# Weighing the last 64 rows of a head pair together with the 128 rows in front of them

## The chip, the cores and the metric

The kernel runs on one core of one Trainium2 chip. The metric is the device time of one execution in microseconds (us). Three runs of the kernel before gave 1619.87, 1620.59 and 1620.89 us, a median of 1620.59 us.

## The reference

Eight batches of eight heads, 576 rows, 64 columns per head. Each row of the scores keeps its 32 largest entries; the softmax of those weights the rows of v. The result feeds a gated FFN.

```python
scores = q @ k.T / sqrt(64)                    # (8, 8, 576, 576)
kth = 32nd largest of each row
scores = where(scores >= kth, scores, -1e9)
attn = softmax(scores)                         # exp(s - max) / (sum + 1e-9)
x = (attn @ v) -> (8 * 576, 512)
out = (sigmoid(x @ w_gate) * (x @ w_val)) @ w_out    # d_model 512, d_ff 1536
```

## The kernel before

Two heads are worked on together as a pair p (four pairs in a batch). A batch has 576 = 4 * 128 + 64 rows, so a pair has five row tiles: i = 0 to 3 of 128 rows for each of both heads, and i = 4, whose 64 rows of the one head and 64 rows of the other fill one tile of 128 partitions. Work goes in steps, one (group, pair, tile) each. `groups` (line 57) halves a batch: an even batch into tiles 0, 1, 2 and tiles 3, 4; an odd one into tiles 0, 1 and tiles 2, 3, 4. Each half is walked pair by pair.

A step loads queries (`ask`), makes scores on TensorE (PE) (`scores`, evicted by ScalarE (ACT), line 226), finds the 32nd largest value on VectorE (DVE) with ACT and GpSimd (POOL) (`select`), and makes masked numerators e and the reciprocal of their sum, inv, spread over the partitions (`masked`). Two steps later come the two functions of this change. `turn` transposes e on PE in chunks of 128 keys into PSUM tiles pt (two buffers, `ps_t`) and ACT copies these into the tile et, whose slots 0 to 3 hold the first head's keys, 5 to 8 the second's, and slot 4 the last 64 keys of both. A tile with i < 4 takes nine transposes (line 321) and three copies (line 322); the last one takes four transposes (326) and a copy of 128x512 (327), then one transpose (329) and a copy of 64 partitions (330). `weigh` multiplies et with the values vt into one PSUM bank po (one buffer, `ps_o`). For n of 128 or 256 columns: eight products with 64 weight columns, alternating between the upper and the lower half of the output partitions (lines 340, 341), and a full one with the mixed chunk (342). For the last tile, n = 64: eight such products (345, 346), then two of 64 rows by 64 columns, a quarter of the array each (347, 348). Products of float32 appear as two PE instructions each. Then inv is transposed into the same bank (351), ACT copies that to rs (354), DVE multiplies po by rs into xf (357, or twice on 64 partitions in 361), ACT makes the rounded part xh (364) and POOL the rest xl (365), in one or two pieces, as the units of 384 columns are cut.

The calls of `weigh` per pair: in an even batch tiles 0 and 1 together (n = 256), tile 2 (128), tile 3 (128), tile 4 (64); in an odd batch tiles 0 and 1 (256), tiles 2 and 3 (256), tile 4 (64). That makes 48 calls of 256 columns, 32 of 128 and 32 of 64 in all.

The FFN runs in twelve units of 384 columns (`ffn`, lines 396 to 398 for gate and val, 415 to 417 for the output). It is written into the program between the steps as a `goal` in worked columns allows, and the last unit after the last step. Weights are split into two parts in the first group of steps (`split_weight`). Within these data dependences the order of each engine's instructions is not that of the code: line 593 lets the tile framework order them by a timeline that it simulates while it builds the program.

Of the kernel before, what the change touches and what calls it, by code (L numbers as in the profile page):

```python
# [16 lines left out]
ALU = mybir.AluOpType  # L17
# [11 lines left out]
def tile_topk_attention_then_gated_ffn(  # L29
# [143 lines left out]
        return ks  # L173

    def load_values(b, p, nm):
        vt = bv.tile([P, 11, D], F32, tag="v", name=f"v_{nm}")
        nc.sync.dma_start(vt, v[b, p].rearrange("p (c d) -> p c d", d=D))
        return vt

# [133 lines left out]
    def turn(e, i, et, o, nm):  # L313

        ef = e.rearrange("p j s -> p (j s)")
        if i < NT:
            for g in range(3):
                pt = ps_t.tile([P, 4, P], F32, tag="t", name=f"pt_{nm}_{g}")
                for c in range(3):
                    k0 = (3 * g + c) * P  # L320
                    nc.tensor.transpose(pt[:, c], ef[:, k0 : k0 + P], ident)  # L321
                nc.scalar.activation(et[:, 3 * g : 3 * g + 3, o : o + P], pt[:, :3], AF.Copy)  # L322
        else:
            pt = ps_t.tile([P, 4, P], F32, tag="t", name=f"pt_{nm}_0")
            for c in range(4):
                nc.tensor.transpose(pt[:, c], ef[:, c * P : (c + 1) * P], ident)
            nc.scalar.activation(et[:, :4, :P], pt, AF.Copy)
            pt = ps_t.tile([P, 4, P], F32, tag="t", name=f"pt_{nm}_1")
            nc.tensor.transpose(pt[:REM, 0], ef[:, NT * P : S], ident)
            nc.scalar.activation(et[:REM, 4, :P], pt[:REM, 0], AF.Copy)  # L330

    def weigh(et, vt, n, invs, pieces, nm):

        both = ps_o.tile([P, 4 * P], F32, tag="o", name=f"po_{nm}")
        po, rb = both[:, :n], both[:, 2 * P :]
        if n > REM:
            mixed = vt[:, 4:6].rearrange("p a d -> p (a d)")

            for c in reversed(range(4)):
                nc.tensor.matmul(po[D:], vt[:, 6 + c], et[:, 5 + c, :n], start=c == 3, stop=False)  # L340
                nc.tensor.matmul(po[:D], vt[:, c], et[:, c, :n], start=c == 3, stop=False)
            nc.tensor.matmul(po, mixed, et[:, 4, :n], start=False, stop=True)  # L342
        else:
            for c in range(4):
                nc.tensor.matmul(po[:D], vt[:, c], et[:, c, :REM], start=c == 0, stop=False)
                nc.tensor.matmul(po[D:], vt[:, 6 + c], et[:, c, REM:P], start=c == 0, stop=False)
            nc.tensor.matmul(po[:D], vt[:REM, 4], et[:REM, 4, :REM], start=False, stop=True)
            nc.tensor.matmul(po[D:], vt[:REM, 10], et[:REM, 4, REM:P], start=False, stop=True)

        for t, inv in enumerate(invs):  # L350
            nc.tensor.transpose(rb[:, t * P : (t + 1) * P], inv, ident)  # L351
        rs = b2.tile([P, 2 * P], F32, tag="rs", name=f"rs_{nm}")
        m = len(invs) * P
        nc.scalar.activation(rs[:, :m], rb[:, :m], AF.Copy)
        xf = b2.tile([P, 2 * P], F32, tag="xf", name=f"xf_{nm}")[:, :n]
        if n > REM:
            nc.vector.tensor_tensor(xf, po, rs[:, :n], op=ALU.mult)
        else:
            for h in range(2):
                d = slice(h * D, h * D + D)  # L360
                nc.vector.tensor_tensor(xf[d], po[d], rs[d, h * REM : h * REM + REM], op=ALU.mult)
        o = 0
        for (xh, xl), c, k in pieces:
            nc.scalar.activation(xh[:, c : c + k], xf[:, o : o + k], AF.Copy)
            nc.gpsimd.tensor_tensor(xl[:, c : c + k], xf[:, o : o + k], xh[:, c : c + k], op=ALU.subtract)  # L365
            o += k
# [61 lines left out]
    def run(general):  # L428
        steps = [(g, p, i) for g, (_, first, end) in enumerate(groups) for p in range(NP) for i in range(first, end)]
        keys, values, qs, staged, xs = {}, {}, {}, {}, {}  # L430
        mark = "g" if general else ""

        def fetch(m):
            if m < len(steps) and steps[m][2] == groups[steps[m][0]][1]:
                g, p, _ = steps[m]
                b, first, _ = groups[g]
                if first == 0:
                    keys[b, p] = load_keys(b, p, f"{mark}{g}_{p}")
                values[g, p] = load_values(b, p, f"{mark}{g}_{p}")

        def begin(m):
            if m < len(steps):
                g, p, i = steps[m]
                staged[m] = scores(qs.pop(m), keys[groups[g][0], p], i, f"{mark}{groups[g][0]}_{i}_{p}")

        def ask(m):
            if m < len(steps):
                g, p, i = steps[m]
                qs[m] = load_queries(groups[g][0], i, p)

        for m in range(max(FETCH, ASK)):
            if m < FETCH:
                fetch(m)
            if m < ASK:
                ask(m)
        for m in range(AHEAD):
            begin(m)
        todo, work, at, col, unit = [], 0, 0, 0, 0
        parts, done = {}, {}

        for n in range(len(steps) + 2):
            if n < len(steps):
                g, p, i = steps[n]
                b, first, end = groups[g]
                m = n

                if not general and g == 0:
                    early, steps0 = LOADED + HELD, 3 * NP
                    for t in range(n * early // steps0, (n + 1) * early // steps0):
                        split_weight(order[t], t >= LOADED)  # L470
                        stored.add(order[t])
                fetch(n + FETCH)
                ask(n + ASK)
                begin(n + AHEAD)
                J = 2 if i < NT else 1
                nm = f"{mark}{b}_{i}_{p}"
                if general:
                    parts[n] = select_any(J, staged.pop(n), nm)
                else:
                    parts[n] = select(J, staged.pop(n), col, nm)  # L480
                next(parts[n])
                col += J
            if n - 1 in parts:
                done[n - 1] = next(parts.pop(n - 1))

            goal = max(at - BEHIND, min((at - U) * 1.5, U)) * 3 * (2 * NF * NP + NE * NF)
            while todo and work < goal:
                cost = next(todo[0], None)
                if cost is None:
                    todo.pop(0)  # L490
                else:
                    work += cost
            if n < 2:
                continue
            g, p, i = steps[n - 2]
            b, first, end = groups[g]
            nm = f"{mark}{b}_{i}_{p}"
            e, inv = done.pop(n - 2)
            if i == first or (i - first) % 2 == 0 or i == NT:
                et, o, invs = b2.tile([P, 9, 2 * P], F32, tag="et", name=f"et_{nm}"), 0, []  # L500
            turn(e, i, et, o, nm)
            invs.append(inv)
            o += P if i < NT else REM
            if len(invs) == 2 or i >= end - 1 or i == NT - 1:

                t, left, pieces = b * S + (i + 1 - len(invs)) * P, o, []
                while left:
                    u, c = t // U, t % U
                    if (u, p) not in xs:
                        if u % 3 == 2 and len(bxs) == 1:  # L510

                            for _ in todo.pop(0) if todo else ():
                                pass
                            split_done()
                        xs[u, p] = [bxs[u % 3 // 2].tile([P, U], F32R, tag=k, name=f"{k}{mark}_{u}_{p}") for k in ("xh", "xl")]
                    k = min(left, U - c)
                    pieces.append((xs[u, p], c, k))
                    t, left = t + k, left - k
                weigh(et, values[g, p], o, invs, pieces, nm)
            at += (P if i < NT else REM) / NP  # L520
            if p == NP - 1 and i == end - 1:
                while (unit + 1) * U <= b * S + min(end * P, S):
                    todo.append(ffn(f"{mark}{unit}", [xs[unit, d] for d in range(NP)], unit * U, general))
                    unit += 1
        for rest in todo:
            for _ in rest:
                pass
# [69 lines left out]
```

## Time and profile before

| | before |
|---|---|
| median of 3 runs | 1620.59 us |
| profiled execution | 1619.79 us |
| its span, first to last instruction | 1618.0 us |
| PE busy | 1553.3 us (96%) |
| DVE busy | 1265.3 us (78%) |
| POOL busy | 1206.8 us (75%) |
| ACT busy | 1168.9 us (72%) |
| mean granted PE clock | 0.981 of full speed |

A busy time is the sum of the times in which an engine had an instruction in work. Matmuls are pipelined: the record of one lasts longer than the distance to the next, so what one costs a full PE is read from the chain of waits, where a piece runs from the end of the piece before it to its own end.

### The profile page before, as it was taken

The page shows a single profiled execution, that of the slowest core. Times are in us where ns is not written, and L with a number is a line of the kernel's source. Part 1 is how long each engine was busy: PE and PEld are TensorE (multiplying, and loading weights), DVE is VectorE, ACT ScalarE, POOL GpSimd, SP SyncE. Part 2 cuts the span into 40 slices and gives each one's busy share as a digit, 9 for nine tenths or more (in the row PEclk, how much of TensorE's full clock was granted, in tenths as well). Part 3 has the DMA queues.
Part 4 walks back from the last instruction along what each step waited for, and adds up shares of the span by engine and source line. Part 5 has one row for each costly group of instructions (what it writes and reads, how often), then busy time and mean ns, then how long its engine had stood idle before and what let it go on. Part 6 is the DMA issues. An engine that isn't in the chain of part 4 may idle for free.

```text
span 1618.0 us, 33444 instructions
## 1 busy us (share of the span) xinstructions
PE 1553.3 (96%) x10226; PEld 1391.1 (86%) x10226; DVE 1265.3 (78%) x5748; ACT 1168.9 (72%) x2615; POOL 1206.8 (75%) x1923
## 2 busy tenths in 40 slices
PE   5878999899999999999999999999999999999998
PEld 2434897789999999999999999989999999999998
DVE  5999878988888779887888778888788778888300
ACT  6888778977777777777777777777777777777322
POOL 3679977897767896787877886788876996776413
PEclk9878999999999999999999999999999999999999
DMA  7556745665655565565555665655565665554575
GB/s 240 191 187 223 262 166 190 208 217 207 220 191 187 197 247 198 207 227 204 200 193 189 222 234 188 218 175 206 202 200 181 217 225 197 187 200 165 194 268 178
DMA packets 88989, 331.98 MB, mean 205 GB/s; under 512 B 9952, under 2 KB 36576, under 8 KB 61920
## 3 DMA queue, kind: packets, MB, share of 16 engines
q1 hardware_dynamic: 88800, 329.75, 59.0%
q8 instruction: 83, 1.36, 0.3%
q14 instruction: 106, 0.87, 0.2%
HBM read 301.40 MB, written 28.31 MB: 204 GB/s over the span
## 4 chain that ended last, share of the span: by engine, by line
PE 75%; POOL 7%; DVE 4%; ACT 3%; issue 1%; DMA 1%; POOLq 0%; SPq 0%; ACTq 0%
PE pz L396 11%; PE pz L397 11%; PE pz L398 11%; PE pss L219 8%; PE pt L321 6%; PE po L340 6%; PE po L415 5%; PE po L417 5%; PE po L416 5%; POOL u L302 3%; PE po L342 2%; DVE e L238 1%; PE po L351 1%; POOL k L171 1%; DVE kths L310 1%
## 5 line engine op out<-in xcount | busy, mean ns | idle before, releaser
L302 POOL TENSOR_TENSOR u<-s,under 128x288 f32<-128x288 f32 x576 | 444.5, 794 | 83.3 <-ACT under L296 77.3
L284 DVE MAX8 cand<-s 128x8 f32<-128x72 f32 x2304 | 348.1, 218 | 73.4 <-ACT s L226 63.3
L396 PE MATMUL pz<-xh,w 128*128 128x384 f32 x1120 | 383.9, 344 | 0.5 <-ACT gf L401 0.5
L397 PE MATMUL pz<-xl,w 128*128 128x384 f32 x1120 | 380.1, 339 | 0.3 <-POOL xl L365 0.3
L398 PE MATMUL pz<-xh,w 128*128 128x384 f32 x1120 | 379.5, 339 | 0.0
L238 DVE SCALAR_TENSOR_TENSOR e<-s,kths,e 128x576 f32<-128x576 f32 x288 | 291.7, 1020 | 2.8 <-ACT e L233 2.7
L310 DVE MAX8 kths<-u 128x8 f32<-128x584 f32 x288 | 219.6, 763 | 88.5 <-POOL u L303 86.3
L296 ACT ACTIVATE under<-s,leads 128x576 bf16<-128x576 f32 x288 | 223.4, 777 | 43.1 <-DVE leads L288 38.1
L233 ACT ACTIVATE e<-s,st 128x576 f32<-128x576 f32 x288 | 210.1, 774 | 52.0 <-POOL st L292 51.3
L404 POOL TENSOR_TENSOR gl<-gf,gh 128x384 fp32r<-128x384 f32 x144 | 156.0, 1084 | 92.4 <-ACT gh L403 90.3
L322 ACT ACTIVATE et<-pt 128x384 f32<-128x384 f32 x384 | 179.8, 490 | 46.4 <-PE pt L321 45.8
L396 PEld LDWEIGHTS pz<-xh,w 128*128 128x128 f32 x1120 | 210.8, 188 | 1.7 <-ACT gf L401 1.0
L397 PEld LDWEIGHTS pz<-xl,w 128*128 128x128 f32 x1120 | 211.4, 189 | 1.0 <-POOL xl L365 0.6
L398 PEld LDWEIGHTS pz<-xh,w 128*128 128x128 f32 x1120 | 211.1, 189 | 0.0
L226 ACT ACTIVATE s<-pss 128x576 f32<-128x576 f32 x256 | 164.5, 643 | 42.1 <-PE pss L219 41.4
L416 PE MATMUL po<-gl,w 128*128 128x384 f32 x560 | 189.5, 340 | 0.4 <-POOL gl L404 0.3
L415 PE MATMUL po<-gh,w 128*128 128x384 f32 x560 | 188.8, 350 | 0.9 <-ACT acc L419 0.9
L321 PE MATMUL pt<-ident,e 128*128 128x128 f32 x1152 | 184.9, 279 | 4.9 <-DVE e L238 2.6
L417 PE MATMUL po<-gh,w 128*128 128x384 f32 x560 | 187.4, 338 | 0.0
L321 PEld LDWEIGHTS pt<-ident,e 128*128 128x128 f32 x1152 | 144.7, 143 | 28.9 <-DVE e L238 6.5
L219 PE MATMUL pss<-k,qh 128*128 128x288 f32 (+2 forms) x588 | 167.5, 303 | 2.0 <-ACT s L226 2.0
L219 PE MATMUL pss<-k,ql 128*128 128x288 f32 (+2 forms) x588 | 159.1, 293 | 0.0
(105 smaller groups left out, 3318.6 us busy)
## 6 DMA issues: line engine op xcount, KB each, us to landing
w<-ws SPq DMA_DIRECT2D x210, 1024.0 KB, 4.9
v<-in_v_dram SPq DMA_DIRECT2D x64, 352.0 KB, 3.3
wraw<-in_w_dram SPq DMA_DIRECT2D x36, 512.0 KB, 4.4
ws<-wsplit SPq DMA_DIRECT2D x36, 512.0 KB, 3.5
qraw<-in_q_dram SPq DMA_DIRECT2D x140, 128.0 KB, 3.0
kraw<-in_k_dram SPq DMA_DIRECT2D x56, 288.0 KB, 3.8
out_dram<-acc SPq DMA_DIRECT2D x48, 192.0 KB, 4.0
q<-in_q_dram SPq DMA_DIRECT2D x20, 128.0 KB, 3.5
```

Source lines behind the costliest of these rows:

```text
L219: nc.tensor.matmul(ps[:, half, o : o + n], x[:K, h * P : (h + 1) * P], ks[h][:K, k0 : k0 + n], start=t == 0, stop=t == len(todo) - 1,)
L238: nc.vector.scalar_tensor_tensor(e[:, j], s[:, j], kth[j], e[:, j], op0=ALU.is_ge, op1=ALU.mult, accum_out=st[:, 4 + j : 5 + j])
L284: nc.vector.max(cand[:, j, 8 * g : 8 * g + 8], s[:, j, g * SEG : (g + 1) * SEG])
L302: nc.gpsimd.tensor_tensor(u[:, j, c], s[:, j, c], under[:, j, c], op=ALU.mult)
L310: nc.vector.max(kths[:, at[j] : at[j] + 8], u[:, j])
L321: nc.tensor.transpose(pt[:, c], ef[:, k0 : k0 + P], ident)
L396: nc.tensor.matmul(ps, wt[:, u, 0, d], xh, start=d == 0, stop=False)
L397: nc.tensor.matmul(ps, wt[:, u, 0, d], xl, start=False, stop=False)
L398: nc.tensor.matmul(ps, wt[:, u, 1, d], xh, start=False, stop=d == NP - 1)
L415: nc.tensor.matmul(ps, wt[:, e % 2, 0, f], gh, start=f == 0, stop=False)
L416: nc.tensor.matmul(ps, wt[:, e % 2, 0, f], gl, start=False, stop=False)
L417: nc.tensor.matmul(ps, wt[:, e % 2, 1, f], gh, start=False, stop=f == FG - 1)
```

## The change

The last tile no longer has a weigh call of its own. Its transposes are written behind the 128 columns of tile 3 in the same et, and one call weighs 192 columns. Tile 2 of an odd batch, which shared a call with tile 3, is weighed alone. The calls per pair become 256, 128 and 192 columns in every batch, 32 of each in all. For the last tile to have the layout of the others, `turn` copies each half of the 128 rows to the slots of its head (two copies of 128 partitions by 4 times 64), transposes the last 128 key columns once more as a whole, and copies 64x64 of each of the last two transposes to slot 4. The values lose their eleventh chunk, which was a second copy of the second head's first 64 rows at partitions 0 to 63.

```diff
-        vt = bv.tile([P, 11, D], F32, tag="v", name=f"v_{nm}")
+        vt = bv.tile([P, 10, D], F32, tag="v", name=f"v_{nm}")
...
-            nc.scalar.activation(et[:, :4, :P], pt, AF.Copy)
+            for h in range(2):
+                nc.scalar.activation(et[:, 5 * h : 5 * h + 4, o : o + REM], pt[:, :, h * REM : h * REM + REM], AF.Copy)
             pt = ps_t.tile([P, 4, P], F32, tag="t", name=f"pt_{nm}_1")
             nc.tensor.transpose(pt[:REM, 0], ef[:, NT * P : S], ident)
-            nc.scalar.activation(et[:REM, 4, :P], pt[:REM, 0], AF.Copy)
+            nc.tensor.transpose(pt[:, 1], ef[:, S - P : S], ident)
+            for h in range(2):
+                d = slice(h * D, h * D + D)
+                nc.scalar.activation(et[d, 4, o : o + REM], pt[d, h, h * REM : h * REM + REM], AF.Copy)
...
-        if n > REM:
-            mixed = vt[:, 4:6].rearrange("p a d -> p (a d)")
-
-            for c in reversed(range(4)):
-                nc.tensor.matmul(po[D:], vt[:, 6 + c], et[:, 5 + c, :n], start=c == 3, stop=False)
-                nc.tensor.matmul(po[:D], vt[:, c], et[:, c, :n], start=c == 3, stop=False)
-            nc.tensor.matmul(po, mixed, et[:, 4, :n], start=False, stop=True)
-        else:
-            for c in range(4):
-                nc.tensor.matmul(po[:D], vt[:, c], et[:, c, :REM], start=c == 0, stop=False)
-                nc.tensor.matmul(po[D:], vt[:, 6 + c], et[:, c, REM:P], start=c == 0, stop=False)
-            nc.tensor.matmul(po[:D], vt[:REM, 4], et[:REM, 4, :REM], start=False, stop=True)
-            nc.tensor.matmul(po[D:], vt[:REM, 10], et[:REM, 4, REM:P], start=False, stop=True)
+        mixed = vt[:, 4:6].rearrange("p a d -> p (a d)")
+
+        for c in reversed(range(4)):
+            nc.tensor.matmul(po[D:], vt[:, 6 + c], et[:, 5 + c, :n], start=c == 3, stop=False)
+            nc.tensor.matmul(po[:D], vt[:, c], et[:, c, :n], start=c == 3, stop=False)
+        nc.tensor.matmul(po, mixed, et[:, 4, :n], start=False, stop=True)
...
-        if n > REM:
-            nc.vector.tensor_tensor(xf, po, rs[:, :n], op=ALU.mult)
-        else:
+        f = n // P * P
+        nc.vector.tensor_tensor(xf[:, :f], po[:, :f], rs[:, :f], op=ALU.mult)
+        if n > f:
             for h in range(2):
                 d = slice(h * D, h * D + D)
-                nc.vector.tensor_tensor(xf[d], po[d], rs[d, h * REM : h * REM + REM], op=ALU.mult)
+                nc.vector.tensor_tensor(xf[d, f:], po[d, f:], rs[d, f + h * REM : f + h * REM + REM], op=ALU.mult)
...
-            if i == first or (i - first) % 2 == 0 or i == NT:
+            if i == NT - 1 or (i < NT and (i - first) % 2 == 0):
                 et, o, invs = b2.tile([P, 9, 2 * P], F32, tag="et", name=f"et_{nm}"), 0, []
...
-            if len(invs) == 2 or i >= end - 1 or i == NT - 1:
+            if len(invs) == 2 or i == end - 1 or i == NT - 2:
...
-    vl = np.zeros((B, H // 2, P, 11, D), v.dtype)
+    vl = np.zeros((B, H // 2, P, 10, D), v.dtype)
...
-    vl[:, :, :R, 10] = vb[:, :, :R]
-    vl = vl.reshape(B, H // 2, P, 11 * D)
+    vl = vl.reshape(B, H // 2, P, 10 * D)
```

## Rows read from the trace of the kernel before

**Rows 1.** Busy time of each engine in three stretches of the span: start and end, length, then busy us and number of instructions for each engine, the granted PE clock, the DMA share and GB/s.

```profile
0.00:200.00 200.00, 156.76 (x727) 93.27 (x728) 171.23 (x747) 158.20 (x325) 142.84 (x233) 0.87 0.66 221
200.00:1530.00 1330.00, 1315.29 (x9038) 1217.94 (x9037) 1086.87 (x4987) 990.85 (x2249) 1039.58 (x1666) 1.00 0.58 202
1530.00:1618.00 88.00, 81.21 (x465) 79.88 (x463) 7.24 (x15) 19.81 (x42) 24.35 (x25) 0.99 0.62 222
```

**Rows 2.** The waits of PE between 200 and 1530 us: who waited for whom, us in total, times, longest.

```profile
PE pt L321 <- ACT et L322: 2.2, 1, 2.2
...
PE po L340 <- DVE xf L357: 1.7, 1, 1.7
```

**Rows 3.** The chain of waits through a weigh call of 256 columns, in order of time: start, us, engine, tile, line. After it one transpose of the last tile and the next FFN product.

```profile
1521.60 0.36 PE po L340
1521.97 0.21 PE po L340
...
1523.48 0.63 PE po L342 x2
1524.11 0.22 PE po L351 x2
1524.33 0.11 PE pt L329
1524.44 0.18 PE pz L397
```

**Rows 4.** The same chain through a call of 128 columns.

```profile
824.72 0.25 PE po L340
...
825.74 0.42 PE po L342 x2
826.16 0.11 PE po L351
826.27 0.27 PE pss L219 x2
```

**Rows 5.** The same chain through a call of 64 columns.

```profile
1480.67 0.20 PE po L345
1480.87 0.05 PE po L345
...
1481.28 0.20 PE po L347
...
1481.54 0.26 PE po L351
1481.80 0.66 PE pt L321 x6
```

**Rows 6.** The quarter-array products of line 347 in the first two of the same three stretches: PE busy us and count, weight loads, clock, DMA share, GB/s. A call has two of them.

```profile
0.00:200.00 200.00, 0.33 (x2) 0.19 (x2) 0.87 0.66 221
200.00:1530.00 1330.00, 10.06 (x62) 5.82 (x62) 1.00 0.58 202
```

**Rows 7.** Groups of instructions by line and shape: line, engine, operation, tiles, shapes, count | busy us, mean ns of one | idle before, releaser. First PE, then the weight loads of line 340.

```profile
L329 PE MATMUL pt<-ident,e 128*64 128x128 f32 x32 | 8.7, 272 | 0.0
L340 PEld LDWEIGHTS po<-et,v 128*64 128x64 f32 x640 | 77.2, 139 | 43.6 <-issue 10.7 <-ACT et L322 3.0 <-DVE xf L357 2.0
```

**Rows 8.** The same view for ACT, DVE and POOL.

```profile
L327 ACT ACTIVATE et<-pt 128x512 f32<-128x512 f32 x32 | 19.0, 595 | 5.4 <-PE pt L326 5.4
L330 ACT ACTIVATE et<-pt 64x128 f32<-64x128 f32 x32 | 8.4, 261 | 0.0
L354 ACT ACTIVATE rs<-po 128x256 f32<-128x256 f32 x48 | 18.2, 379 | 20.2 <-PE po L351 20.1
L354 ACT ACTIVATE rs<-po 128x128 f32<-128x128 f32 x64 | 17.3, 270 | 15.7 <-PE po L351 15.3
L364 ACT ACTIVATE xh<-xf 128x64 fp32r<-128x64 f32 x48 | 12.2, 257 | 12.1 <-DVE xf L361 12.0
L364 ACT ACTIVATE xh<-xf 128x128 fp32r<-128x128 f32 x32 | 10.0, 313 | 10.5 <-DVE xf L357 10.5
L364 ACT ACTIVATE xh<-xf 128x192 fp32r<-128x192 f32 x16 | 5.9, 370 | 2.4 <-DVE xf L357 2.1
L357 DVE TENSOR_TENSOR xf<-po,rs 128x128 f32<-128x128 f32 x32 | 8.8, 276 | 1.6 <-ACT rs L354 1.5
L365 POOL TENSOR_TENSOR xl<-xf,xh 128x64 fp32r<-128x64 f32 x48 | 20.2, 421 | 4.4 <-ACT xh L364 3.6
L365 POOL TENSOR_TENSOR xl<-xf,xh 128x192 fp32r<-128x192 f32 x16 | 10.5, 659 | 1.5 <-ACT xh L364 1.0
```

**Rows 9.** The DMA of the values (queue, count, KB each, median us from issue to landing).

```profile
v<-in_v_dram SPq DMA_DIRECT2D x64, 352.0 KB, 3.3
```

**Rows 10.** The timeline of POOL after the last weigh call: start, us, line, tiles.

```profile
1532.08 0.32 POOL L365 TENSOR_TENSOR xl<-xf,xh 128x64 fp32r<-128x64 f32 x1
```

**Rows 11.** The chain of waits at the first product of the last FFN unit.

```profile
1535.67 0.17 PE pz L396
```

**Rows 12.** ACT in order of time near a weigh call of 64 columns: start, us, line, tiles [idle before, releaser].

```profile
1480.15 0.78 ACT L296 ACTIVATE under<-s,leads 128x576 bf16<-128x576 f32 x1 [0.43 <-DVE leads L288]
```

## The prediction

> **What bounds the kernel now.** I read first how the busy time lies in the span. In the first 200 us PE is busy 156.76 of 200 and DVE 171.23: several engines wait for each other there, and time taken from PE is worth little. From 200 to 1530 us PE is busy 1315.29 of 1330 us at a granted clock of 1.00, while DVE has 1086.87, POOL 1039.58 and ACT 990.85 [rows 1]. What fills PE there sets the end; the other engines have 243, 290 and 339 us to spare. After 1530 us only the FFN is left. Second, PE's waits in the long stretch: its whole idle time is 1330 - 1315.3 = 14.7 us, and the waits that touch this change happened once each, 2.2 us for a copy into et and 1.7 us for xf [rows 2]. Third, the chain of waits through the calls. This view is needed because the mean of a PE record is no price: the transpose of line 329 lasts 272 ns by its record [rows 7], but its piece of the chain is 0.11 us, and the product behind it has 0.18 us [rows 3]. So every PE price below is a stretch of the chain, from the start of a call's first piece to the start of what follows the call.
>
> **Where the calls lie.** Of the 64 quarter-array products of line 347, two to a call, 2 lie before 200 us and 62 after [rows 6]. So 31 of the 32 small calls stand where PE is full, and one, of batch 0, does not. I count nothing for that one.
>
> **PE, the calls.**
> - 256 columns with two transposes of inv: 1521.60 to 1524.33, 2.73 us [rows 3].
> - 128 columns with one: 824.72 to 826.27, 1.55 us [rows 4].
> - 64 columns with one: 1480.67 to 1481.80, 1.13 us [rows 5]. Much of it isn't work on columns. The first piece is 0.20 where a later one of line 345, with its partner, is 0.06; the first quarter product is 0.20 again; the transpose behind it is 0.26 where 0.11 is usual. That is 0.14 + 0.14 + 0.15 = 0.43 us for three changes of how the array is divided. A call without quarters has two of them: 0.36 for 0.21 at its start and 0.63 for 0.43 at line 342, 0.15 + 0.20 us [rows 3].
> - 192 columns with two transposes of inv: not in the trace. Without the transposes the calls of 256 and 128 cost 2.73 - 0.22 = 2.51 and 1.55 - 0.11 = 1.44; both have the same 18 products and the same two changes, so what differs is the columns, and 192 is the mean, 1.975. With two transposes 2.195 us. The ends are the two neighbours, 1.44 + 0.22 = 1.66 and 2.73. I take the mean, because the price of a piece goes with its columns (0.06, 0.11, 0.21 for 64, 128, 256).
>
> Even batch, per pair: before 1.55 + 1.13 = 2.68, after 2.195, a gain of 0.485. Odd batch: before 2.73 + 1.13 = 3.86, after 1.55 + 2.195 = 3.745, a gain of 0.115; the columns are the same 320, only the changes of the array go, and one call more ends on the dear line 342. Sum: 15 * 0.485 + 16 * 0.115 = 7.3 + 1.8 = 9.1 us.
>
> **PE, the added transpose.** One more full transpose for each last tile, 31 * 0.11 = 3.4 us by the chain [rows 3]. The nearest row from the other side is the record, 0.272 us [rows 7], 8.4 us. I take 0.11, since in the chain the next product is not late behind it. Net on PE: 9.1 - 3.4 = 5.7 us gained.
>
> The Trainium skill speaks against this choice: its page "TensorE: Matmul & The Clock Gate" (Part 4: PE-mode transpose) measures about 275 ns for a 128x128 transpose in a kernel's context. By that price the sum would be 9.1 - 31 * 0.275 = 0.6 us. The record in this trace agrees with the page (272 ns), the distance to the next product (0.11 us) does not.
>
> **ACT.** Per last tile, copies of 595 and 261 ns go [rows 8]. In their place come two copies of 256 elements a partition, for which the nearest is rs of that size, 379 ns, and two of 64 elements, at most the 257 ns of xh 128x64: 1272 for 856 ns, 0.42 us, 13.3 us in all. In an even batch a copy of rs of 379 stands for two of 270, and one of xh of 370 for 313 and 257 [rows 8]: 16 * 0.36 = 5.8 us less. Net 7.5 us of ACT, hidden in its 339 spare us; if ACT were the bound, it would cost that. Below: its records overlap at their ends, so 0 is possible. I take nothing.
>
> **DVE, POOL.** In an odd batch the product po * rs is cut in two, at most one more of 276 ns, 16 * 0.28 = 4.4 us of DVE [rows 8] against 243 spare. POOL has one xl less per pair of an even batch. Both hidden; nothing, with ends of 0 and 4.4 us.
>
> **The values.** Each of 64 loads shrinks by a tenth of 3.3 us at the most [rows 9], 0.3 us each. They are issued two steps ahead, and PE has no wait for them between 200 and 1530 us. Their queue, SP, carries nothing new. Nothing, with at most a few us of gain in the first 200 us as the other end.
>
> **The wait that is added.** Tile 3 is now weighed only when tile 4 has been transposed and copied, one step later. Behind a weigh call that comes too early stand, on PE, the next FFN products and the next transposes, and behind those ACT's copies. But et has two buffers and needs no more of them than before, and the FFN of those columns is put into the program only after the group's last pair. At the very end the last xl is done at 1532.08 + 0.32 = 1532.40 [rows 10], and the last FFN unit starts at 1535.67 [rows 11]: 3.27 us of slack. The last call is later by 2.195 - 1.13 = 1.07 on PE, 0.11 for the transpose, 0.42 for the copies, 0.11 for rs, 0.28 on DVE, 0.11 for xh and 0.24 for xl [rows 8]: 2.3 us. It fits, with 0.9 us left.
>
> **The sum.** The profiled execution took 1619.79 us, 1.79 more than its span. Less 5.7 that is 1614.1 us. The median of the runs is 0.8 us above the profiled one, so I predict 1614.9 us. By the ends of the transposes alone (0.11 or 0.272 us) it is 1614.9 to 1619.9 us. A call of 192 at its lower end of 1.66 us would give 31 * 0.535 = 17 us more, one at 2.73 us would take as much; both would need 64 columns to be free or dear as 128, against all three sizes, and stay outside the range.
>
> **Rivals.**
> - *The transposes cost their records.* Then 9.1 - 8.4 = 0.7 us is left and the time is 1619.9 us, no change. For it: 272 ns [rows 7]. Against it: the chain [rows 3]. Chance 0.06.
> - *The new order of the program gives the gain back.* The tile framework orders the instructions by its own simulated timeline, and every price in that has changed a little. PE's 14.7 us of idle time are made of waits that happened once or a few times [rows 2], accidents of one order. With 4 us more of them the time is 1618.9 us, no change measured. Against it: it can as well lose some of them. Chance 0.18.
> - *The call of 192 waits for its own tile.* Place: PE at the first product of line 340, since the order was laid for one copy of 64 partitions and now four copies stand behind whatever ACT has begun. Price: a piece of ACT such as the sign pass of 0.78 us [rows 12]; at every second call 16 * 0.78 = 12.5 us, time 1614.9 + 12.5 = 1627.4 us, slower. It eats the whole gain from 5.7 / 32 = 0.18 us per call and makes the kernel measurably slower from (5.7 + 3.2) / 32 = 0.28 us. Against it: so far the weight loads of line 340 waited 3.0 us for et in 80 calls, 0.04 us a call [rows 7]. Chance 0.08.
> - *The change does not do what it says:* one PE piece of a last tile too many or few would show in the counts; I see none in the diff and give it no chance of its own.
>
> **How the numbers follow.** My forecast has 0.68, with a range of its own of 1610 to 1617 us: an order that loses 4 to 5 us of the idle time below, one that adds 2 above. A measurement of this kernel tells about 0.2% from no change, 3.2 us. The forecast is faster by more than that (below 1617.3). The rivals of the transposes and of the order, 0.24 together, lie within 0.2%; the waiting call, 0.08, is slower. The range for 8 in 10 goes from 1609.5 to 1621 us: it takes in both rivals without a change and leaves out the slower one and the far ends of the order.
>
> **What would show it.** Right: lines 345 to 348 gone, the chain through a call of 192 columns near 2.2 us with its two transposes, the added transpose at 0.11 us of chain, PE busy between 200 and 1530 us still at 99% with the same FFN work, and the last unit's start some 5.7 us earlier. Wrong: a wait of PE or its weight loads at line 340 for et that is counted in tens, a call of 192 that is well above 2.2 us, or named waits of PE that add up to 4 us more than before although the calls are as cheap as worked out; then the order and not the operations decided.

## The result, and the profile after

The changed kernel took 1629.74 us in the median of 6 runs (1627.32 to 1634.33), the kernel before, on the same chip beside it, 1620.74 us. The ratio is 1.0052 (95% interval 1.0034 to 1.0070): slower by 8.4 us where 5.7 us of gain were forecast. The profiled execution took 1627.84 us, its span is 1626.0 us.

The same three stretches of the span as in [rows 1], of the changed kernel (PE, weight loads, DVE, ACT, POOL, then the granted clock):

```profile
0.00:200.00 200.00, 153.11 (x675) 88.36 (x676) 167.30 (x731) 154.75 (x320) 137.68 (x226) 0.87 0.66 215
200.00:1530.00 1330.00, 1308.06 (x8717) 1216.24 (x8716) 1092.68 (x5016) 993.25 (x2284) 1033.60 (x1656) 0.99 0.58 200
1530.00:1626.00 96.00, 89.24 (x518) 87.02 (x516) 7.99 (x17) 21.09 (x44) 25.98 (x27) 0.98 0.61 224
```

PE is idle 21.9 us between 200 and 1530 us where it was 14.7, and 46.9 us before 200 us where it was 43.2. Over the whole span PE is busy 1550.4 us (1553.3 before): it does a little less, and it stands 10.9 us more (75.6 us for 64.7).

First the priced pieces. The chain of waits through a call of 192 columns, to be held against [rows 3, 4]:

```profile
1511.44 0.31 PE po L343
1511.75 0.01 PE po L344
1511.76 0.16 PE po L343
...
1512.89 0.52 PE po L345 x2
1513.42 0.22 PE po L348 x2
1513.64 0.66 PE pt L321 x6
```

From 1511.44 to 1513.64 it takes 2.20 us; 2.195 were worked out. The same chain through the last tile's transposes (line 331 is the added one), and the group of the added ones:

```profile
1504.74 0.44 PE pt L326 x4
1505.18 0.11 PE pt L330
1505.29 0.11 PE pt L331
```

```profile
L331 PE MATMUL pt<-ident,e 128*128 128x128 f32 x32 | 8.7, 272 | 0.0
```

Again 0.11 us in the chain under a record of 272 ns. The Trainium skill's figure of about 275 ns (page "TensorE: Matmul & The Clock Gate", Part 4: PE-mode transpose) agrees with the record of one and not with what one more of them costs a full PE.

Summed over the trace, each PE record from the end of the one before to its own end, idle time left out, the products and inv transposes of `weigh` take 213.7 us for 224.9, and the added transposes 3.5: the operations are 7.7 us cheaper. So the time must have gone to waits and to the clock. The longest waits of PE, over the whole span:

```profile
PE wrest L146 <- DVE wraw L139: 15.9, 8, 6.0
PE pt L321 <- DVE e L238: 11.1, 6, 5.1
PE pss L203 <- DMA q<-in_q_dram: 6.4, 1, 6.4
PE pt L321 <- ACT et L322: 5.7, 7, 1.3
PE pss L219 <- ACT s L226: 5.5, 9, 2.0
...
PE po L343 <- ACT et L322: 1.3, 3, 0.5
...
PE po L343 <- ACT et L328: 0.7, 1, 0.7
```

The same rows of the kernel before:

```profile
PE pt L321 <- DVE e L238: 2.6, 4, 0.8
PE pt L321 <- ACT et L322: 2.2, 1, 2.2
PE pss L219 <- ACT s L226: 2.0, 2, 1.8
```

No call waits for its own tile to any account: line 343 waits 2.0 us for et in four places. What grew are the waits of transposes and scores for the attention's other engines: in the kernel before the transposes waited 2.2 us for et and the scores 2.0 us for s (once or twice), now 5.7 and 5.5 us in 7 and 9 places. The largest growth, of the transposes' wait for e from 2.6 to 11.1 us, lies in the first 200 us, where other waits shrank. By stretches PE's idle time grew by 3.7 us before 200 us, by nothing from 200 to 345 us and by 7.3 us from 345 to 1600 us.

The places show more; the largest growth in one of them after 345 us lies near 1420 us. Busy times in stretches of 10 us there, the changed kernel first, then the kernel before:

```profile
1410.00:1420.00 10.00, 10.00 (x70) 9.14 (x66) 7.41 (x32) 7.88 (x19) 7.27 (x13) 1.00 0.56 183
1420.00:1430.00 10.00, 8.00 (x50) 7.00 (x50) 8.13 (x41) 6.16 (x14) 8.52 (x15) 0.91 0.52 180
1430.00:1440.00 10.00, 8.07 (x54) 5.78 (x51) 8.67 (x44) 7.78 (x18) 5.10 (x12) 0.84 0.18 49
```

```profile
1420.00:1430.00 10.00, 10.00 (x66) 8.39 (x65) 6.97 (x36) 6.39 (x15) 9.31 (x16) 1.00 0.80 253
1430.00:1440.00 10.00, 10.00 (x66) 9.89 (x65) 9.13 (x48) 6.99 (x16) 4.59 (x10) 1.00 0.67 238
```

In 20 us PE stands 3.9 us, and the clock is granted at 0.91 and 0.84, means of its two levels of 2.4 and 1.2 GHz (1.00 and 0.50). The chain of waits through that place:

```profile
1421.99 0.24 DVE leads L288
...
1422.32 0.87 ACT under L296 x2
1423.18 0.76 ACT et L322 x2
1423.94 0.84 ACT e L233 x2
...
1425.16 0.86 ACT under L296 x2
1426.02 0.30 ACT qh L188
1426.33 0.55 ACT s L226
...
1426.92 1.48 PE pss L219 x10
1428.40 0.62 PE po L343
1429.02 0.01 PE po L344
1429.02 0.42 PE po L343
```

For a while the chain isn't on PE: ACT works off a queue, PE waits 2.0 us for one of its copies, then a piece of 256 columns takes 0.42 us where 0.21 is usual [rows 3], that is, 1.2 GHz for 2.4.

Why here: the columns of FFN unit 10 reach into tiles 0 and 1 of batch 7, so it needs the 256-column calls of all four pairs. PE in order of time, the changed kernel first (unit 10's first product, the first score product after the wait, the call of the fourth pair, the next product of unit 10), then the kernel before:

```profile
1418.03 0.33 PE L393 MATMUL pz<-xh,w 128*128 128x384 f32 x1
...
1426.92 0.40 PE L219 MATMUL pss<-k,qh 128*128 128x288 f32 x1 [2.00 <-ACT s L226]
...
1428.33 0.69 PE L343 MATMUL po<-et,v 128*64 128x256 f32 x1
...
1436.45 0.79 PE L393 MATMUL pz<-xh,w 128*128 128x384 f32 x3 [1.25 <-ACT xh L361]
```

```profile
1420.59 0.33 PE L396 MATMUL pz<-xh,w 128*128 128x384 f32 x1
...
1422.24 0.43 PE L340 MATMUL po<-et,v 128*64 128x256 f32 x1
```

Before, the fourth pair's call follows 1.7 us after unit 10's first product. In the changed kernel it follows 10.3 us after; by 1424.6 us PE has done the 27 FFN products that three pairs allow (three PSUM tiles, nine products each). Then no FFN work is left, and PE hangs on DVE, ACT and POOL, step by step. Counted in the trace, PE has done 1266 score products when unit 10 starts at 1420.6 us in the kernel before, but only 1248 when it starts at 1418.0 us in the changed kernel: the FFN has run further ahead of the attention. After a third of unit 10 both have done 1304 score products, at 1462.0 and at 1469.6 us: the stretch is 10.2 us longer, partly by the 18 score products and what follows from them, and by 3.9 us idle and (0.09 + 0.16) * 10 = 2.5 us of clock.

### The profile page after: what moved, and what is told of

It reads as the page before. It is cut to its first block, busy times and chain, and to the rows that moved or that the text cites. A ratio compares the mean times of both kernels' runs of the same rounds, so it can differ in the third digit from the quotient of the medians.

```text
span 1626.0 us, 32812 instructions
## 1 busy us (share of the span) xinstructions
PE 1550.4 (95%) x9906; PEld 1391.6 (86%) x9906; DVE 1268.0 (78%) x5764; ACT 1169.1 (72%) x2647; POOL 1197.3 (74%) x1907
## 3 DMA queue, kind: packets, MB, share of 16 engines
q1 hardware_dynamic: 88800, 327.65, 58.5%
## 4 chain that ended last, share of the span: by engine, by line
PE 59%; DVE 11%; POOL 10%; ACT 10%; issue 3%; DMA 3%; POOLq 0%; SPq 0%; ACTq 0%; DVEq 0%
PE pz L394 9%; PE pz L395 9%; PE pz L393 9%; PE pss L219 7%; PE po L343 5%; PE pt L321 4%; POOL u L302 4%; PE po L412 4%; PE po L413 4%; PE po L414 4%; DVE e L238 3%; DVE kths L310 3%; DVE cand L284 2%; ACT e L233 2%; ACT under L296 2%
## 5 line engine op out<-in xcount | busy, mean ns | idle before, releaser
L302 POOL TENSOR_TENSOR u<-s,under 128x288 f32<-128x288 f32 x576 | 438.8, 784 | 103.1 <-ACT under L296 99.0
L238 DVE SCALAR_TENSOR_TENSOR e<-s,kths,e 128x576 f32<-128x576 f32 x288 | 296.0, 1033 | 3.8 <-ACT e L233 2.0
L401 POOL TENSOR_TENSOR gl<-gf,gh 128x384 fp32r<-128x384 f32 x144 | 153.0, 1064 | 89.5 <-ACT gh L400 86.4
L321 PE MATMUL pt<-ident,e 128*128 128x128 f32 x1152 | 181.9, 279 | 17.0 <-DVE e L238 11.1
```

Source lines behind the costliest of these rows:

```text
L238: nc.vector.scalar_tensor_tensor(e[:, j], s[:, j], kth[j], e[:, j], op0=ALU.is_ge, op1=ALU.mult, accum_out=st[:, 4 + j : 5 + j])
L302: nc.gpsimd.tensor_tensor(u[:, j, c], s[:, j, c], under[:, j, c], op=ALU.mult)
```

## The experiments

Theories: the order of the instructions (C), the joined call itself (D), and as a first form of C the shorter load of the values (A), since the order differs from that of the kernel before from 33 us on, long before the first joined call. B, in the first four texts, stands for all that isn't A. Each ratio is to the kernel before, run beside it.

### The load of the values, and the two halves of the change

e1 is the changed kernel that loads the eleventh chunk again, though nothing reads it:

```diff
-        vt = bv.tile([P, 10, D], F32, tag="v", name=f"v_{nm}")
+        vt = bv.tile([P, 11, D], F32, tag="v", name=f"v_{nm}")
...
```

> The changed kernel with the eleventh chunk of the values loaded again (read by nothing). The order of the program then stays that of the kernel before through the first steps, up to the first last tile; in the changed kernel it differs from the first 30 us on. Theory A (the shorter load shifts the order from the start, and that costs the time): 1615 us, the 5.7 us of the forecast come back. Theory B (the joined call itself makes PE wait, or the order after it is worse): 1627 to 1631 us, as the changed kernel. In between: both.

Measured: 1627.84 us, ratio 1.0027 (1.0013 to 1.0040). e2 is the kernel before with ten chunks:

```diff
-        vt = bv.tile([P, 11, D], F32, tag="v", name=f"v_{nm}")
+        vt = bv.tile([P, 10, D], F32, tag="v", name=f"v_{nm}")
...
-            nc.tensor.matmul(po[D:], vt[:REM, 10], et[:REM, 4, REM:P], start=False, stop=True)
+            nc.tensor.matmul(po[D:], vt[:REM, 5], et[:REM, 4, REM:P], start=False, stop=True)
...
```

> The kernel before with the ten-chunk load alone; the last tile's product of the second head reads chunk 5 at partitions 0 to 63 instead of chunk 10, so that head's first 64 keys are left out for the last 64 rows, at the same instructions. Theory A: about 1629 us or more, since the load alone makes the order worse (the 9 us lost, without the 5.7 won). Theory B: 1620 us as before.

Measured: 1623.31 us beside 1622.87, 1.0002 (0.9991 to 1.0014). So the load alone costs nothing. In the changed kernel the eleventh chunk brings some 4 us by the ratios (1.0052 and 1.0027, whose intervals overlap) and 1.9 us by the medians; A had expected 1615 us. Theory A falls as the whole cause. e3 and e4 join the calls in one kind of batch, with eleven chunks as in e1:

```diff
# e3, even batches
-            if i == first or (i - first) % 2 == 0 or i == NT:
+            if i == first or (i - first) % 2 == 0:
...
-            if len(invs) == 2 or i >= end - 1 or i == NT - 1:
+            if len(invs) == 2 or i == end - 1:
# e4, odd batches
-            if i == first or (i - first) % 2 == 0 or i == NT:
+            if i == first or i == 2 or i == 3 or (i == NT and b % 2 == 0):
...
-            if len(invs) == 2 or i >= end - 1 or i == NT - 1:
+            if len(invs) == 2 or i == end - 1 or (i == NT - 2) or (i == NT - 1 and b % 2 == 0):
```

(Both take the new copies where the last tile joins, the old ones where not.)

> The joined call in the even batches only, where tiles 3 and 4 stand in a group of their own; odd batches as before (256 and 64), eleven chunks. By the forecast's prices PE gains 15 * 0.485 - 15 * 0.11 = 5.6 us, nearly the whole gain: 1615 us if the order costs nothing. Theory A (early load): 1615 us. Theory B (the joined call waits): about half of the loss, 1622 to 1625 us.

> The joined call in the odd batches only (128 and 192 for 256 and 64); even batches as before, eleven chunks. PE gains 16 * 0.115 - 16 * 0.11 = 0.1 us: 1621 us if the order costs nothing and by theory A. Theory B: 1624 to 1629 us, the other half of the loss or all of it.

Measured: even 1621.10 us, 0.9985 (0.9975 to 0.9995); odd 1619.99 us, 0.9975 (0.9965 to 0.9986). Both are faster than the kernel before, but not by the prices: the even half gains 2.4 us where 5.6 were priced, the odd half 4.1 where 0.1 was. With both halves joined and eleven chunks the ratio is 1.0027 (e1). A cost that comes with each joined call doesn't make 16 calls of each kind faster and 32 of both slower, which speaks against theory D in its simple form. It is no proof, since orders alone differ by as much (below). What is left is the order.

### Holding the FFN back, and letting it ahead

e5 leaves every operation and changes from batch 6 on how far the FFN is held behind the attention:

```diff
-            goal = max(at - BEHIND, min((at - U) * 1.5, U)) * 3 * (2 * NF * NP + NE * NF)
+            late = 24 if b >= 6 else 0
+            goal = max(at - BEHIND - late, min((at - U) * 1.5, U)) * 3 * (2 * NF * NP + NE * NF)
```

> The changed kernel, with the FFN held back by 24 more columns from batch 6 on; operations the same, and the order of the program the same up to unit 8. In the changed kernel PE starts FFN unit 10 at 1418 us with 18 score products fewer behind it than the kernel before, then runs out of FFN work: 3.9 us idle from 1420 to 1440 us at a granted clock of 0.91 and 0.84, some 6.4 us. Theory C (the order lets the FFN run ahead, and PE is starved at the start of unit 10): the stall goes, 1623 us. Theory D (the joined call itself makes PE wait): 1628 to 1630 us, unchanged.

> The same hold of 24 columns in the changed kernel with eleven chunks (e1, 1627.8 us). Theory C: 1621.4 us, level with the kernel before or a little below. Theory D: 1628 us.

> The kernel before, without the joined call, with the FFN let ahead by 16 columns from batch 6 on; the order is the same up to unit 7, and unit 10 starts with 14 score products fewer done. Theory C: the kernel before gets the same stall, 5 us slower, 1626 to 1628 us. Theory D: no stall without a joined call, 1621 to 1623 us.

(e6 has the same line with eleven chunks, e7 -16 for 24 in the kernel before. The score products in these texts and in those that follow are counted in the order as built; the counts are 84 lower throughout than in the traces, 1164 for 1248 and 1182 for 1266.) Measured: e5 1623.35 us, 1.0013 (1.0001 to 1.0024); e6 1621.03 us, 0.9991 (0.9979 to 1.0003); e7 1625.62 us, 1.0016 (1.0006 to 1.0026). The stretch from 1420 to 1440 us, e5 first, then e7:

```profile
1420.00:1440.00 20.00, 20.00 (x144) 18.61 (x143) 16.67 (x78) 12.93 (x32) 16.96 (x28) 1.00 0.68 234
```

```profile
1420.00:1440.00 20.00, 17.68 (x106) 15.82 (x106) 17.12 (x82) 14.00 (x31) 13.71 (x25) 0.91 0.50 167
```

With the hold the idle time is gone and the clock stays at 1.00; by the ratios 6.3 us (e5) and 5.8 us (e6 against e1) are won, 6.4 had been worked out. In the kernel before, without any joined call, letting the FFN ahead makes PE stand 2.3 us at the same place, at 0.91 of the clock; it costs 2.6 us, half of the 5 that I had expected. So this stall is made by how far the FFN has run ahead of the attention when unit 10 becomes due. That is shown from both sides, and the traces of all twenty kernels agree. Where unit 10 starts with 1248 score products done (the changed kernel, e1, e11), PE stands 3.9 to 5.2 us from 2 us before that start to 30 us behind it; with 1252 (e7) 2.3 us; with 1256 (e4, e9, e10, e13, e18) 0 to 1.0 us; with 1266 or more (the other eleven) at most 0.3 us.

The stall isn't the whole loss: e5 is rid of it and comes out level with the kernel before, not 5.7 us below it.

e8 holds all batches back by 500 columns (BEHIND = 500 for 480):

> The changed kernel with the FFN held back by 500 columns for 480 in all batches. Unit 10 then starts with as many score products done as in the kernel before, so by theory C the late stall goes, 1623 us; the order changes from unit 3 on as well, which can add or take some us (1620 to 1627). Theory D: 1628 to 1630 us.

Measured: 1623.86 us, 1.0010 (0.9998 to 1.0022), as theory C had it.

### Does the saved PE time come out over several orders?

The same constant in both kernels gives pairs with the same operations in another order.

```diff
-    BEHIND = 480
+    BEHIND = 500
```

> The kernel before with the FFN held back by 500 columns for 480: same operations, another order. Pair of e8. Theory C (the joined call gains its 5.7 us, the order scatters by some us either way): 1623.9 + 5.7 = 1629.6 us, give or take 4 us of scatter. Theory D (the joined call gains nothing by itself): 1624 us.

> The kernel before with the FFN held back by 460 columns. In the order as built, unit 10 then starts with 1172 score products done for 1182, unit 4 with 492 for 510. Theory C: some stall at the start of those units, 1624 to 1629 us. If the order were of no weight: 1622.6 us, as before.

> The changed kernel with 460 columns, the pair of e10; unit 10 starts with 1164 score products done, as in the changed kernel itself, so it should keep the stall there. Theory C: 5.7 us less than e10 on the mean of such pairs, with 4 us of scatter: 1619 to 1628 us. Theory D: as e10 or above.

> The changed kernel with the FFN held back by 520 columns. Accident of the order: on the mean of the pairs 5 us below its partner e14. Idle grows with the gain: level with e14. Work of PE at full clock: 1520 us by either theory.

> The kernel before with 520 columns: 1622 to 1626 us, as at 480 and 500; work of PE at full clock 1527 us.

> The changed kernel with 540 columns; unit 10 starts with 1186 score products done for 1164, and each unit from 3 on with more than in the kernel before. Accident of the order: 1617 to 1621 us, below its partner e16 by 5 us on the mean. Idle grows with the gain: level with e16.

> The kernel before with 540 columns: 1622 to 1626 us; work of PE at full clock 1527 us, and idle after 345 us of 5 to 11 us as in the other orders without the joined call.

| hold, columns | before: ratio | joined: ratio | difference, us |
|---|---|---|---|
| 460 (e10, e11) | 1.0046 | 1.0060 | +2.3 |
| 480 (the two kernels) | 1 | 1.0052 | +8.4 |
| 500 (e9, e8) | 1.0014 | 1.0010 | -0.6 |
| 520 (e14, e13) | 1.0020 | 1.0022 | +0.3 |
| 540 (e16, e15) | 0.9998 (0.9989 to 1.0008) | 0.9977 (0.9966 to 0.9987) | -3.4 |

(The difference is that of the ratios times 1622.) The kernel before alone moves by 7.8 us between holds. The pairs differ by -3.4 to +8.4 us, 1.4 us slower on the mean. The interval of each ratio is some 0.1% to either side, up to 0.2% in the first two rows, so only the differences at 480 and at 540 columns stand clear of the noise. Of the expectations, e10 (1628.83 us), e14 (1625.47), e15 (1617.62) and e16 (1621.43) came within 1 us of their ranges; e9 (1623.50) was 6 us below mine and e11 (1630.75) above its range, since both took the 5.7 us for given in each pair. These two came out as theory D had it, which in this form says that the joined call gains nothing by itself. e13 took 1625.56 us, level with e14, as "idle grows with the gain" had it; e15, 3.8 us below e16, is nearer to "accident of the order". So the pairs don't decide whether idle time is an accident of the order or grows with the gain.

Where the gain goes is read from PE's time, from its records and those of the clock. For each profiled execution: PE busy with the part at the half clock counted half (the work at full clock); the part at the half clock; and PE's idle time to 345 us (the last weights are split by 325 us) and from there to 1600 us. All in us.

| | work at full clock | busy at the half clock | idle to 345 us | idle from 345 to 1600 us |
|---|---|---|---|---|
| no joined call: before, e2, e7, e9, e10, e14, e16 | 1524.2 to 1529.3, mean 1526.7 | 46.7 to 53.7, mean 49.9 | 52.4 to 57.1, mean 55.2 | 5.5 to 10.7, mean 8.1 |
| joined in all batches: after, e1, e5, e6, e8, e11, e12, e13, e15, e17 | 1517.8 to 1522.6, mean 1519.8 | 52.1 to 64.1, mean 57.5 | 53.5 to 58.5, mean 56.0 | 7.4 to 17.8, mean 10.5 |

The work falls by 6.9 us on the mean, and the two ranges don't touch; in the five pairs of the same hold it falls by 3.1 to 7.2 us, 5.3 on the mean, against 5.7 forecast. Idle time takes back 3.2 us of the 6.9 on the mean and 9 in one order (e11, 72.6 us in all against 63.3). The clock takes back as much again: 7.7 us more of PE's work is done at the half clock, which costs 3.8 us. Together that is the whole gain, and the mean spans, 1621.7 and 1622.0 us, agree. Most of the work at the half clock (38 to 54 us) lies in the first 200 us, and one execution of each kernel is a small sample; over all runs the granted clocks of the two groups average 0.981 and 0.979. The profiled execution of the kernel before, on which I forecast, has the least idle time of all seventeen in both stretches.

### Versions that are faster than both

e12 has eleven chunks and a longer hold from batch 4 on; e17 is e1 and e18 is e4 with BEHIND = 540:

```diff
+            late = 48 if b >= 4 else 0
```

> The changed kernel with eleven chunks and 48 more columns of hold from batch 4 on, so that both unit 7 and unit 10 start with more score products done (850 and 1186 for 832 and 1164). e6 (hold in batches 6 and 7 alone) still had 4.9 us of idle PE at the start of unit 7. Theory C: 2 to 4 us below e6 (1621.0), 1617 to 1619 us, faster than the kernel before and the changed one. Theory D: as e6 or above.

> The changed kernel with eleven chunks and 540 columns of hold. Eleven chunks gave 2 to 2.5 us twice (e1 against the changed kernel, e6 against e5). If that adds to e15 (1617.6 us): 1615 us. If the order decides anew, anything from 1616 to 1624 us; unit 10 starts with 1186 score products done, unit 7 with 836, so a stall at unit 7 as in e6 would be no surprise.

> The joined call in odd batches alone with 540 columns. PE's work gains next to nothing by the forecast's prices (0.1 us). Order alone: 1618 to 1626 us. The call's gain alone, over e16 (1621.4): 1621 us.

Measured: e12 1619.92 us, 0.9984 (0.9975 to 0.9994), 1 us below e6 where 2 to 4 were expected; e17 1618.88 us, 0.9978 (0.9966 to 0.9989), no better than e15, so the eleven chunks don't add once the order is another; e18 1617.71 us, 0.9971 (0.9961 to 0.9981), the best. Against e16 (0.9998) the odd half gains 4.4 us, though its operations were priced at nothing; its work at full clock is 1523.5 us, 3.2 below the mean of the kernels without a joined call but only 0.7 below e16's. I had expected 1621 for the call alone and 1618 to 1626 for the order, and it came out just below both; which of the two it is, the runs don't tell.

## Why the prediction was wrong

- *The calls and the transposes:* right. 2.20 us for 2.195, 0.11 for 0.11, and 5.5 us of PE's work at full clock gone between the two kernels (1527.0 and 1521.5 us) for the 5.7 of the sum. The Trainium skill (page "TensorEngine Tiling (Array Packing)", Key Properties) says that a change of the tiling mode drains TensorE. The 0.14 us and more at each change of how the array is divided agree with it [rows 3, 5].
- *ACT, DVE, POOL, the values' load:* none became a bound. ACT is busy 1169.1 us in all, as before (1168.9). The load by itself made no difference (e2, 1.0002).
- *The wait that is added:* right; line 343 waited 2.0 us for et, and the tail held, for PE is busy without a gap from 1450 to 1600 us.
- *"What fills PE there sets the end"*, and with it the step from PE's work to the time, failed. It holds for most of the time between the starts of units, not behind some of them: in the changed kernel 9.9 of the 12.8 us of idle time between 345 and 1600 us come within 51 us of the starts of units 4, 7 and 10, whose columns reach into tiles 0 and 1 of an odd batch. There the FFN work that fills PE's gaps can run out, as read for unit 10, and the attention's chain through ACT, DVE and POOL is the bound. A microsecond taken from PE's work before such a point is worth nothing if it is then waited for. Of the 14.7 us of idle time in the kernel before I took the waits as accidents that would stay as many, and the clock at no cost; they are what moves. The account of the two profiled executions closes: 5.5 us less work, 10.9 us more idle time, and 2.7 us for 5.5 us more work at the half clock (57.9 for 52.4) make 8.1 us, and the span grew by 8.0. The profile showed the place: the score products waited 1.8 us at 1064 us and the transposes 2.2 at 1059, just after unit 7 had started.
- *The order.* I named it as a rival with 4 us and a chance of 0.18. Idle time grew by 10.9 us in the profiled executions (58.0 to 68.8 us up to 1530 us), of which 3.9 us stand at the start of unit 10, with 2.5 us of clock; that stall, 6.4 us, is shown to be the order's (e5, e7). For the other 7 us, half of them in the first 200 us, no run shows the cause. The sign that I had named came: calls as cheap as worked out, and named waits of PE that add up to 10 us more. The rival's mechanism was right for the part that is shown; its size was off, its sign was left at either way, and it stood at the weight of a side case although the change touches the load that every step's order depends on.
- *The range.* 1609.5 to 1621 us rested on an order that adds 2 us at the most inside my own case. Seven orders of the kernel before spread over 7.8 us with PE's operations unchanged, and the execution on which I forecast was the one with the least idle time; that is the width that a change of this size meets.

Open: why the two halves of the change are each faster and both together, at 480 columns, slower; and whether idle time and work at the half clock grow because PE's work shrinks or because these ten orders happened to be worse. The means of the idle time differ by 3.2 us, which is less than the spread of single orders.

## What to carry to other kernels

A microsecond of work taken from the busiest engine is worth a microsecond only where other work stands ready to fill the place; look for the points at which that filler becomes due (here the start of an FFN unit), and read the waits just behind them. Where a tool lays the order from its own timeline, a small edit re-lays all of it: measure how far the time moves when one neutral constant changes, before crediting or blaming the edit. Then tune that constant together with the edit: the joined call was 1.0052 at one value and 0.9977 at another.

## What the runs showed of the hardware

PE stood 2.0 and 1.9 us in two stretches of 10 us, and its granted clock in them was 0.91 and 0.84, where the stretch before, without idle time, had 1.00. The pieces of a 256-column call then took 0.42 us for 0.21, the lower of the two levels. I had priced idle time at its own length; here 3.9 us of it brought 2.5 us of clock with it. With the idle time gone (e5) the clock stayed at 1.00 there.
